# Transposing packed pairs of bf16 as 4-byte elements on TensorE, with the DMA transposes moved back there, in an attention and token-mixing kernel

## The chip, the cores and the metric

The kernel runs on one core of one Trainium2 chip. The metric is the device time of one execution in microseconds (us); several executions are timed and the median of all of them is quoted, slow ones included. Executions are sorted into a fast and a slow state by their length and by TensorE's granted clock (0.968 to 1.00 over the runs of this study); only fast ones are compared, unless it is said otherwise. Each batch of experiments has its own runs of the kernel before, on the same chip; their median is 182.5, 182.8 or 183.6 us.

## The reference

Retention with a decaying state per head (4 batches, 8 heads of 64, 768 steps), then a token-mixing block:

```python
for t in range(S):
    state = gamma * state + outer(k[t], v[t])       # per batch and head
    y[t] = scale * q[t] @ state
x = y with the heads side by side                    # [4, 768, 512]
theta = x @ w_theta
y = w_tok_r @ (x * cos(theta)) + w_tok_i @ (x * sin(theta))
u = x + y
out = u + max(u @ w_ch, 0)                           # float32
```

The kernel cuts time into 24 chunks of 128 rows (6 per batch), works on bf16 copies, and computes retention in blocks. It needs five kinds of transpose: of k and q, of the retention output x, of the token weights w, and of u.

## The kernel before

A transpose on TensorE is one matmul with an identity and a copy out of PSUM. k and q lie side by side in one bf16 tile:

```python
def att_T(n):                                  # k, q of a chunk on TensorE
    kq_ps = psum.tile([P, 2 * NP, P], BF, name="kq_ps", tag="tr", bufs=2)
    for i, src in enumerate((s["kb"], s["qb"])):
        for j in range(NP):                    # NP = 4: eight transposes
            nc.tensor.transpose(kq_ps[:, i * NP + j, :], src[:, j * P:(j + 1) * P], ident)
    kqT = work.tile([P, 2 * NP, P], BF, name="kqT", bufs=4)
    nc.vector.tensor_copy(kqT, kq_ps)

def att_T_dma(n):                              # the same by a DMA
    kqT = work.tile([P, 2 * NP, P], BF, name="kqT", bufs=4)
    nc.sync.dma_start_transpose(out=kqT, in_=s["kqb"].rearrange("p a d -> p (a d)"))
```

Two constants choose where a transpose is done. Chunks from `N_DMA` on transpose k, q and x by DMA, row blocks from `M_DMA` on transpose u by DMA; everything earlier is on TensorE:

```python
N_DMA = (B - 1) * nT + 1      # 19 of 24 chunks: 5 kq and 5 x go by DMA
M_DMA = (B - 2) * nT          # 12 of 24 blocks: u of 12..22 goes by DMA
```

The end is a routine of its own. With u by DMA, the loop runs the product `moe_O` one slot late, so the routine has to add it for blocks 21 and 22:

```python
def moe_last(m):              # m = 23
    ...
    moe_U_dma(m - 1)          # transpose u of block 22
    prods(0)                  # first half of block 23's token mix
    moe_O(m - 2)              # output product of block 21
    prods(1)
    flip(0); moe_O(m - 1); flip(1)
    ...                       # 8 products of 256 columns, two outputs
```

The main loop takes one chunk and one or two half groups of token-mix products (`moe_M`, six 512-column products each) per slot.

Of the kernel before, what the change touches and what calls it, by code (L numbers as in the profile page):

```python
# [32 lines left out]
def kernel(  # L33
# [17 lines left out]
    nc = tc.nc  # L51
# [10 lines left out]
    N_DMA = (B - 1) * nT + 1  # L62
    M_DMA = (B - 2) * nT
# [64 lines left out]
    ident = const.tile([P, P], BF)  # L128
# [13 lines left out]
    wT = [const.tile([P, nT, S], BF, name="wtr"), const.tile([P, nT, S], BF, name="wti")]  # L142
# [4 lines left out]
    def att_prep(n):  # L147
        c = n % nT
        r3 = "p (h d) -> p h d"
        kqb = work.tile([P, 2, dm], BF, name="kqb", bufs=5)  # L150
        kb, qb = kqb[:, 0, :], kqb[:, 1, :]
# [8 lines left out]
    def att_T(n):  # L160
        s = st[n]
        kq_ps = psum.tile([P, 2 * NP, P], BF, name="kq_ps", tag="tr", bufs=2)
        for i, src in enumerate((s["kb"], s["qb"])):
            for j in range(NP):
                nc.tensor.transpose(kq_ps[:, i * NP + j, :],  # L165
                                    src[:, j * P:(j + 1) * P], ident)
        kqT = work.tile([P, 2 * NP, P], BF, name="kqT", bufs=4)
        nc.vector.tensor_copy(kqT, kq_ps)  # L168
        s["kqT"] = kqT

    def att_T_dma(n):
        s = st[n]
        kqT = work.tile([P, 2 * NP, P], BF, name="kqT", bufs=4)
        nc.sync.dma_start_transpose(
            out=kqT, in_=s["kqb"].rearrange("p a d -> p (a d)"))
        s["kqT"] = kqT

    def att_A(n):
        s = st[n]
        kqT = s["kqT"]  # L180
        at_ps = psum.tile([P, 2, NP, P], FT, name="at_ps", tag="at", bufs=1)
        for j in range(NP):
            for par in range(2):
                rows = slice(par * D, (par + 1) * D)
                nc.tensor.matmul(at_ps[:, par, j, :], kqT[rows, j, :],  # L185
                                 kqT[rows, NP + j, :], start=(j == 0),
                                 stop=(j == NP - 1), skip_group_check=True)
# [9 lines left out]
    def att_Yinter(n):  # L197
# [3 lines left out]
        if c > 0:  # L201
            for j in range(NP):
                nc.tensor.matmul(s["yT_ps"][:, j, :], stbd[c % 2][:, j, :],  # L203
                                 s["kqT"][:, NP + j, :], start=(j == 0), stop=False,
                                 skip_group_check=True)

    def att_Y(n):
# [22 lines left out]
        xT = work.tile([P, NP, P], BF, name="xT", bufs=3)  # L230
        nc.scalar.copy(xT, yT_ps)  # L231
# [6 lines left out]
    def att_X_dma(n):  # L238
        b, c = divmod(n, nT)
        nc.sync.dma_start_transpose(  # L240
            out=xs[b][:, c, :].rearrange("p (j e) -> p j e", j=NP),
            in_=st[n]["xT"].rearrange("p j t -> p (j t)"))

    def att_X(n):
        b, c = divmod(n, nT)
        s = st[n]
        if n < N_DMA:
            x_ps = psum.tile([P, NP, P], BF, name="x_ps", tag="tr", bufs=2)
            for j in range(NP):
                nc.tensor.transpose(x_ps[:, j, :], s["xT"][:, j, :], ident)  # L250
        th_ps = psum.tile([P, dm], FT, name="th_ps", tag="acc", bufs=2)
        for j in range(NP):
            nc.tensor.matmul(th_ps, s["xT"][:, j, :], wth[:, j, :], start=(j == 0),  # L253
                             stop=(j == NP - 1))
        if n < N_DMA:
            nc.vector.tensor_copy(xs[b][:, c, :], x_ps.rearrange("p j e -> p (j e)"))
# [14 lines left out]
    def moe_M(m, lo, hi):  # L271
# [8 lines left out]
        for s0 in range(lo, hi):  # L280
            for r in range(2):
                nc.tensor.matmul(y_ps, wT[r][:, s0, t0 * P:(t0 + 1) * P],  # L282
# [7 lines left out]
    def moe_U(m):  # L290
        u_ps = psum.tile([P, nD, P], BF, name="u_ps", tag="tr", bufs=2)
        for j in range(nD):
            nc.tensor.transpose(u_ps[:, j, :], mo[m]["u"][:, j * P:(j + 1) * P], ident)
        uT = work.tile([P, nD, P], BF, name="uT", bufs=3)
        nc.scalar.copy(uT, u_ps)
        mo[m]["uT"] = uT

    def moe_U_dma(m):
        uT = work.tile([P, nD, P], BF, name="uT", bufs=3)
        nc.sync.dma_start_transpose(out=uT, in_=mo[m]["u"])  # L300
        mo[m]["uT"] = uT

    def moe_O(m):
        b, t0 = divmod(m, nT)
        if m >= M_DMA:
# [212 lines left out]
```

## Time and profile before

| | before |
|---|---|
| time, median of 3 runs | 182.69 us (182.03 to 184.78) |
| span of the profiled run | 181.8 us |
| TensorE busy over the span | 157.7 us, 87% |
| transposes on TensorE / by DMA | 352 / 21 |
| stretch to 59 us | loads set the pace, TensorE busy 40.5 us |
| 59 us to some 176 us | TensorE full |

The views that this rests on are in the prediction. Three more lines, of the groups of instructions on the page, are below. Columns: line, engine, operation, out<-in, shape and type, count; then busy us, mean ns of one; then idle time of the engine just before them and what ended most of it.

```profile
L165 PE MATMUL kq_ps<-ident,kqb 128*128 128x128 bf16 x152 | 13.6, 234 | 11.1 <-POOL kqb L153 7.0
L153 POOL CAST kqb<-kf 128x512 bf16<-128x512 f32 x24 | 16.0, 667 | 19.9 <-DMA kf<-in_k_dram 14.1
L231 ACT CAST xT<-yT_ps 128x512 bf16<-128x512 f32 x24 | 14.1, 586 | 19.4 <-PE yT_ps L214 18.1
```

The 234 ns of the first line is the duration of one instruction and not the pace, which the prediction reads from starts.

### The profile page before, as it was taken

To read this page: it belongs to the slowest core of one execution; us is meant where nothing else is said; L and a number is where in the kernel's file an instruction comes from. 1 tells how busy PE (TensorE), PEld (TensorE's weight loads), DVE (VectorE), ACT (ScalarE), POOL (GpSimd) and SP (SyncE) were. 2 spreads that over 40 slices of the span, in tenths; PEclk is the share of its full clock that TensorE was granted. 3 is DMA by queue.
4 is the path that set the end of the run, shared out by engine and by line. 5 is a ranking of instruction groups with operands and counts; after the bars stand their busy time and mean duration, and the time that the engine had idled before them with its cause. 6 is when DMAs were issued, how large, how long until landed. Compare 5 with 4: busy or idle time off the path is not lost.

```text
span 181.8 us, 3528 instructions
## 1 busy us (share of the span) xinstructions
PE 157.7 (87%) x1367; PEld 90.7 (50%) x1392; DVE 104.8 (58%) x146; ACT 74.7 (41%) x140; POOL 79.9 (44%) x104
## 2 busy tenths in 40 slices
PE   0567987897764999999999999999999999999991
PEld 0344655553542655656565565455545544444560
DVE  1264794716822777878676877765645744434442
ACT  4053764821429535647554363356345332200010
POOL 4648677869075768865777847250000000000000
PEclk9999999999999999999999999999999999999997
DMA  6999999999998999999999989984483333334433
GB/s 128 222 316 218 224 276 259 294 288 231 227 259 180 260 243 225 222 272 271 223 228 251 266 208 233 263 151 115 119 112 102 103 97 90 104 93 110 132 105 117
DMA packets 95265, 35.63 MB, mean 196 GB/s; under 512 B 89488, under 2 KB 89744, under 8 KB 95248
## 3 DMA queue, kind: packets, MB, share of 16 engines
q1 hardware_dynamic: 95104, 35.27, 86.4%
q8 instruction: 11, 0.18, 0.5%
q10 hardware_dynamic: 144, 0.13, 0.2%
q14 instruction: 6, 0.05, 0.1%
HBM read 25.69 MB, written 6.29 MB: 176 GB/s over the span
## 4 chain that ended last, share of the span: by engine, by line
PE 62%; SPq 18%; DMA 12%; issue 2%; POOL 2%; DVE 1%; DVEq 0%
PE y_ps L282 27%; SPq L80 15%; PE o_ps L310 11%; PE th_ps L253 8%; DMA kf<-in_k_dram 4%; DMA qf<-in_q_dram 3%; PE yT_ps L214 3%; DMA wtok<-in_moe_w_tok_r_dram 3%; PE at_ps L185 3%; PE kq_ps L165 3%; PE st_ps L222 2%; SPq L94 2%; DMA uT<-u 2%; PE yT_ps L203 2%; PE x_ps L250 1%
## 5 line engine op out<-in xcount | busy, mean ns | idle before, releaser
L282 PE MATMUL y_ps<-z,wti 128*128 128x512 bf16 x137 | 51.9, 379 | 1.6 <-ACT wti L332 0.9
L282 PE MATMUL y_ps<-z,wtr 128*128 128x512 bf16 x125 | 47.4, 379 | 0.7 <-DVE u L287 0.3
L189 DVE TENSOR_TENSOR at<-at_ps,mask 128x1024 bf16<-128x1024 f32 x24 | 29.3, 1220 | 8.9 <-PE at_ps L185 8.8
L258 ACT ACTIVATE cs<-th_ps,halfpi 128x512 bf16<-128x512 f32 x24 | 16.5, 688 | 38.0 <-PE th_ps L253 34.1
L154 POOL TENSOR_TENSOR kqb<-qf,qsc 128x512 bf16<-128x512 f32 x24 | 25.7, 1071 | 11.3 <-DMA qf<-in_q_dram 11.1
L156 POOL TENSOR_TENSOR vb<-vf,vsc 128x512 bf16<-128x512 f32 x24 | 25.9, 1081 | 7.0 <-DMA vf<-in_v_dram 5.8
L264 DVE TENSOR_TENSOR z<-cs,x_sb 128x1024 bf16<-128x1024 bf16 x24 | 19.6, 818 | 14.2 <-ACT cs L259 14.2
L168 DVE COPY kqT<-kq_ps 128x1024 bf16<-128x1024 bf16 x19 | 13.1, 691 | 24.6 <-PE kq_ps L165 24.4
L253 PE MATMUL th_ps<-wth,xT 128*128 128x512 bf16 x89 | 24.4, 387 | 2.4 <-DVE wth L395 1.9
L153 POOL CAST kqb<-kf 128x512 bf16<-128x512 f32 x24 | 16.0, 667 | 19.9 <-DMA kf<-in_k_dram 14.1
L310 PE MATMUL o_ps<-wch,uT 128*128 128x512 bf16 x88 | 23.1, 379 | 0.4 <-DMA uT<-u 0.2
L165 PE MATMUL kq_ps<-ident,kqb 128*128 128x128 bf16 x152 | 13.6, 234 | 11.1 <-POOL kqb L153 7.0
L287 DVE TENSOR_TENSOR u<-y_ps,x_sb 128x512 bf16<-128x512 f32 x23 | 15.8, 690 | 11.9 <-PE y_ps L282 11.9
L313 DVE SCALAR_TENSOR_TENSOR ot<-o_ps,u 128x512 f32<-128x512 f32 x23 | 15.9, 692 | 10.7 <-PE o_ps L310 10.7
L231 ACT CAST xT<-yT_ps 128x512 bf16<-128x512 f32 x24 | 14.1, 586 | 19.4 <-PE yT_ps L214 18.1
L282 PEld LDWEIGHTS <-wti 128*128 128x128 bf16 x138 | 13.5, 98 | 15.4 <-issue 1.9
L282 PEld LDWEIGHTS <-wtr 128*128 128x128 bf16 x138 | 13.5, 98 | 13.5
L165 PEld LDWEIGHTS <-kqb 128*128 128x128 bf16 x152 | 10.6, 104 | 16.5 <-POOL kqb L153 7.9
L259 ACT ACTIVATE cs<-th_ps,zerob 128x512 bf16<-128x512 f32 x24 | 16.3, 681 | 0.0
L236 ACT CAST stbd<-st_ps 64x256 bf16<-64x256 f32 x40 | 14.7, 366 | 0.5
L310 PEld LDWEIGHTS <-uT 128*128 128x128 bf16 x92 | 8.8, 98 | 10.3 <-DMA uT<-u 0.4
L253 PEld LDWEIGHTS <-xT 128*128 128x128 bf16 x96 | 8.8, 100 | 9.2 <-issue 2.6
(51 smaller groups left out, 147.3 us busy)
## 6 DMA issues: line engine op xcount, KB each, us to landing
kf<-in_k_dram SPq DMA_DIRECT2D x24, 256.0 KB, 4.9
qf<-in_q_dram SPq DMA_DIRECT2D x24, 256.0 KB, 5.0
vf<-in_v_dram SPq DMA_DIRECT2D x24, 256.0 KB, 5.3
out_dram<-ot SPq DMA_DIRECT2D x23, 256.0 KB, 2.2
wtok<-in_moe_w_tok_r_dram SPq DMA_DIRECT2D x6, 384.0 KB, 5.3
wtok<-in_moe_w_tok_i_dram SPq DMA_DIRECT2D x6, 384.0 KB, 5.9
w<-in_moe_w_theta_dram SPq DMA_DIRECT2D x1, 1024.0 KB, 6.7
w<-in_moe_w_ch_dram SPq DMA_DIRECT2D x1, 1024.0 KB, 7.8
```

The lines of the kernel that those rows point to most:

```text
L80: nc.sync.dma_start(out=t, in_=src[b, :, c * P:(c + 1) * P, :].rearrange("h s d -> s h d"))
L153: nc.gpsimd.tensor_copy(kb.rearrange(r3, h=H), raw[n, "kf"])
L154: nc.gpsimd.tensor_mul(qb.rearrange(r3, h=H), raw[n, "qf"], _bcast_last(qsc[:, c], D))
L156: nc.gpsimd.tensor_mul(vb.rearrange(r3, h=H), raw[n, "vf"], _bcast_last(vsc[:, c], D))
L165: nc.tensor.transpose(kq_ps[:, i * NP + j, :], src[:, j * P:(j + 1) * P], ident)
L189: nc.vector.tensor_mul(at.rearrange("p a j t -> p (a j) t"), at_ps.rearrange("p a j t -> p (a j) t"), _bcast_mid(mask, H))
L253: nc.tensor.matmul(th_ps, s["xT"][:, j, :], wth[:, j, :], start=(j == 0), stop=(j == NP - 1))
L258: nc.scalar.activation(cs[:, 0, :], th_ps, AF.Sin, bias=halfpi, scale=1.0)
L259: nc.scalar.activation(cs[:, 1, :], th_ps, AF.Sin, bias=zerob, scale=1.0)
L264: nc.vector.tensor_mul(zs[b][:, c], st[n]["cs"], _bcast_mid(xs[b][:, c, :], 2))
L282: nc.tensor.matmul(y_ps, wT[r][:, s0, t0 * P:(t0 + 1) * P], zs[b][:, s0, r, :], start=(s0 == 0 and r == 0), stop=(s0 == nT - 1 and r == 1))
L310: nc.tensor.matmul(o_ps, mo[m]["uT"][:, j, :], wch[:, j, :], start=(j == 0), stop=(j == nD - 1))
```

## The change

Intent: a 4-byte element can carry two bf16 values through a transpose, so half as many transposes do the same work. k and q are interleaved (`[P, dm, 2]`), reinterpreted as float32 and transposed by four instructions instead of eight; x, w and u are packed likewise. Products then read their bf16 operands with a step of two. All 21 DMA transposes return to TensorE.

```diff
-    N_DMA = (B - 1) * nT + 1
-    M_DMA = (B - 2) * nT
...
-    ident = const.tile([P, P], BF)
+    ident = const.tile([P, P], FT)
...
-        kqb = work.tile([P, 2, dm], BF, name="kqb", bufs=5)
-        kb, qb = kqb[:, 0, :], kqb[:, 1, :]
+        kqb = work.tile([P, dm, 2], BF, name="kqb", bufs=5)
+        kb, qb = kqb[:, :, 0], kqb[:, :, 1]
...
     def att_T(n):
-        kq_ps = psum.tile([P, 2 * NP, P], BF, name="kq_ps", tag="tr", bufs=2)
-        for i, src in enumerate((s["kb"], s["qb"])):
-            for j in range(NP):
-                nc.tensor.transpose(kq_ps[:, i * NP + j, :],
-                                    src[:, j * P:(j + 1) * P], ident)
+        kq_ps = psum.tile([P, NP, P], FT, name="kq_ps", tag="tr", bufs=2)
+        for j in range(NP):
+            nc.tensor.transpose(kq_ps[:, j, :],
+                                s["kqb"][:, j * P:(j + 1) * P, :].rearrange(
+                                    "p c i -> p (c i)").bitcast(FT), ident)
+        kqT = work.tile([P, NP, P, 2], BF, name="kqT", bufs=4)
...
+        s["kT"] = [kqT[:, j, :, 0] for j in range(NP)]
+        s["qT"] = [kqT[:, j, :, 1] for j in range(NP)]
-    def att_T_dma(n):
...
-    def att_X_dma(n):
...
-    def moe_U_dma(m):
...
     def moe_last(m):
-        moe_U_dma(m - 1)
+        moe_U(m - 1)
         prods(0)
         moe_O(m - 2)
...
-        if 1 < U_at.get(s_, M_DMA) < M_DMA:
+        if U_at.get(s_, 0) > 1:
             moe_O(U_at[s_])
```

(x, w and u are cut; they follow the same pattern. The cast of w_theta is split between VectorE and ScalarE.) The last two hunks together have a side effect: `moe_O` now runs in the same slot as its transpose, also for block 21, and `moe_last` still runs it a second time.

More of the change, by code (lines that the diff above doesn't have):

```diff
@@ L141 @@
     wch = const.tile([P, nD, dm], BF)
-    wT = [const.tile([P, nT, S], BF, name="wtr"), const.tile([P, nT, S], BF, name="wti")]
+    wT = [const.tile([P, nT, nT // 2, P, 2], BF, name="wtr"),
+          const.tile([P, nT, nT // 2, P, 2], BF, name="wti")]
     st = {}
@@ L161, in att_T @@
         s = st[n]
-        kq_ps = psum.tile([P, 2 * NP, P], BF, name="kq_ps", tag="tr", bufs=2)
-        for i, src in enumerate((s["kb"], s["qb"])):
-            for j in range(NP):
-                nc.tensor.transpose(kq_ps[:, i * NP + j, :],
-                                    src[:, j * P:(j + 1) * P], ident)
-        kqT = work.tile([P, 2 * NP, P], BF, name="kqT", bufs=4)
-        nc.vector.tensor_copy(kqT, kq_ps)
-        s["kqT"] = kqT
-    def att_T_dma(n):
-        s = st[n]
-        kqT = work.tile([P, 2 * NP, P], BF, name="kqT", bufs=4)
-        nc.sync.dma_start_transpose(
-            out=kqT, in_=s["kqb"].rearrange("p a d -> p (a d)"))
-        s["kqT"] = kqT
+        kq_ps = psum.tile([P, NP, P], FT, name="kq_ps", tag="tr", bufs=2)
[4 more added lines that the diff above has]
+        kqT = work.tile([P, NP, P, 2], BF, name="kqT", bufs=4)
+        nc.vector.tensor_copy(kqT.rearrange("p j t i -> p (j t i)"),
+                              kq_ps.rearrange("p j t -> p (j t)").bitcast(BF))
+        s["kT"] = [kqT[:, j, :, 0] for j in range(NP)]
+        s["qT"] = [kqT[:, j, :, 1] for j in range(NP)]
     def att_A(n):
         s = st[n]
-        kqT = s["kqT"]
         at_ps = psum.tile([P, 2, NP, P], FT, name="at_ps", tag="at", bufs=1)
@@ L184, in att_A @@
                 rows = slice(par * D, (par + 1) * D)
-                nc.tensor.matmul(at_ps[:, par, j, :], kqT[rows, j, :],
-                                 kqT[rows, NP + j, :], start=(j == 0),
+                nc.tensor.matmul(at_ps[:, par, j, :], s["kT"][j][rows],
+                                 s["qT"][j][rows], start=(j == 0),
                                  stop=(j == NP - 1), skip_group_check=True)
@@ L203, in att_Yinter @@
                 nc.tensor.matmul(s["yT_ps"][:, j, :], stbd[c % 2][:, j, :],
-                                 s["kqT"][:, NP + j, :], start=(j == 0), stop=False,
+                                 s["qT"][j], start=(j == 0), stop=False,
                                  skip_group_check=True)
@@ L229, in att_Y @@
             zs[b] = big.tile([P, nT, 2, dm], BF, name="z")
-        xT = work.tile([P, NP, P], BF, name="xT", bufs=3)
-        nc.scalar.copy(xT, yT_ps)
+        xT = work.tile([P, NP // 2, P, 2], BF, name="xT", bufs=3)
+        nc.scalar.copy(xT.rearrange("p a t b -> p a b t"),
+                       yT_ps.rearrange("p (b a) t -> p a b t", b=2))
         s["xT"] = xT
@@ L236, in att_Y @@
                 nc.scalar.copy(stbd[(c + 1) % 2][sl, :, sl], st_ps[b][sl, :, sl])
-    def att_X_dma(n):
-        b, c = divmod(n, nT)
-        nc.sync.dma_start_transpose(
-            out=xs[b][:, c, :].rearrange("p (j e) -> p j e", j=NP),
-            in_=st[n]["xT"].rearrange("p j t -> p (j t)"))
     def att_X(n):
@@ L246, in att_X @@
         s = st[n]
-        if n < N_DMA:
-            x_ps = psum.tile([P, NP, P], BF, name="x_ps", tag="tr", bufs=2)
-            for j in range(NP):
-                nc.tensor.transpose(x_ps[:, j, :], s["xT"][:, j, :], ident)
+        x_ps = psum.tile([P, NP // 2, P], FT, name="x_ps", tag="tr", bufs=2)
+        for a in range(NP // 2):
+            nc.tensor.transpose(x_ps[:, a, :],
+                                s["xT"][:, a].rearrange(
+                                    "p t i -> p (t i)").bitcast(FT), ident)
         th_ps = psum.tile([P, dm], FT, name="th_ps", tag="acc", bufs=2)
         for j in range(NP):
-            nc.tensor.matmul(th_ps, s["xT"][:, j, :], wth[:, j, :], start=(j == 0),
-                             stop=(j == NP - 1))
-        if n < N_DMA:
-            nc.vector.tensor_copy(xs[b][:, c, :], x_ps.rearrange("p j e -> p (j e)"))
+            nc.tensor.matmul(th_ps, s["xT"][:, j % 2, :, j // 2], wth[:, j, :],
+                             start=(j == 0), stop=(j == NP - 1))
+        nc.vector.tensor_copy(xs[b][:, c, :],
+                              x_ps.rearrange("p a e -> p (a e)").bitcast(BF))
         cs = work.tile([P, 2, dm], BF, name="cs", bufs=2)
@@ L281, in moe_M @@
             for r in range(2):
-                nc.tensor.matmul(y_ps, wT[r][:, s0, t0 * P:(t0 + 1) * P],
+                nc.tensor.matmul(y_ps, wT[r][:, t0, s0 % (nT // 2), :, s0 // (nT // 2)],
                                  zs[b][:, s0, r, :], start=(s0 == 0 and r == 0),
@@ L290, in moe_U @@
     def moe_U(m):
-        u_ps = psum.tile([P, nD, P], BF, name="u_ps", tag="tr", bufs=2)
-        for j in range(nD):
-            nc.tensor.transpose(u_ps[:, j, :], mo[m]["u"][:, j * P:(j + 1) * P], ident)
-        uT = work.tile([P, nD, P], BF, name="uT", bufs=3)
-        nc.scalar.copy(uT, u_ps)
-        mo[m]["uT"] = uT
-    def moe_U_dma(m):
-        uT = work.tile([P, nD, P], BF, name="uT", bufs=3)
-        nc.sync.dma_start_transpose(out=uT, in_=mo[m]["u"])
-        mo[m]["uT"] = uT
+        u_ps = psum.tile([P, nD // 2, P], FT, name="u_ps", tag="tr", bufs=2)
+        for a in range(nD // 2):
+            nc.tensor.transpose(u_ps[:, a, :],
+                                mo[m]["u"][:, 2 * a * P:2 * (a + 1) * P].bitcast(FT),
+                                ident)
+        uT = work.tile([P, nD // 2, P, 2], BF, name="uT", bufs=3)
+        nc.scalar.copy(uT.rearrange("p a t i -> p (a t i)"),
+                       u_ps.rearrange("p a t -> p (a t)").bitcast(BF))
+        mo[m]["uT"] = [uT[:, j % 2, :, j // 2] for j in range(nD)]
     def moe_O(m):
         b, t0 = divmod(m, nT)
-        if m >= M_DMA:
-            o_ps = psum.tile([P, dm], FT, name="o_ps", tag="tr", bufs=2)
-        else:
-            o_ps = psum.tile([P, dm], FT, name="o_ps", tag="acc", bufs=2)
+        o_ps = psum.tile([P, dm], FT, name="o_ps", tag="acc", bufs=2)
         for j in range(nD):
-            nc.tensor.matmul(o_ps, mo[m]["uT"][:, j, :], wch[:, j, :], start=(j == 0),
+            nc.tensor.matmul(o_ps, mo[m]["uT"][j], wch[:, j, :], start=(j == 0),
                              stop=(j == nD - 1))
         ot = work.tile([P, dm], FT, name="ot", bufs=4)
-        nc.vector.scalar_tensor_tensor(ot, o_ps, 0.0, mo[m]["u"], ALU.max, ALU.add)
+        nc.vector.scalar_tensor_tensor(
+            ot.rearrange("p (b r) -> p b r", b=2),
+            o_ps.rearrange("p (b r) -> p b r", b=2), 0.0,
+            mo[m]["u"].rearrange("p (r b) -> p b r", b=2),
+            ALU.max, ALU.add)
         nc.sync.dma_start(out=out[b, t0 * P:(t0 + 1) * P, :], in_=ot)
@@ L320, in w_cast @@
             row = work.tile([P, S], BF, name="wrow", bufs=3)
-            nc.gpsimd.tensor_copy(row, wdma[r, t0])
+            nc.gpsimd.tensor_copy(
+                row.rearrange("p (i b) -> p b i", b=2),
+                wdma[r, t0].rearrange("p (b i) -> p b i", b=2))
             wrow[r, t0] = row
@@ L325, in w_tok @@
         for r in range(2):
-            w_ps = psum.tile([P, nT, P], BF, name="w_ps", tag="tr", bufs=2)
-            for s0 in range(nT):
-                nc.tensor.transpose(w_ps[:, s0, :],
-                                    wrow[r, t0][:, s0 * P:(s0 + 1) * P], ident)
-            dst = wT[r][:, :, t0 * P:(t0 + 1) * P]
+            w_ps = psum.tile([P, nT // 2, P], FT, name="w_ps", tag="tr", bufs=2)
+            for a in range(nT // 2):
+                nc.tensor.transpose(
+                    w_ps[:, a, :],
+                    wrow[r, t0][:, 2 * a * P:2 * (a + 1) * P].bitcast(FT), ident)
+            dst = wT[r][:, t0].rearrange("p a t b -> p (a t b)")
+            src = w_ps.rearrange("p a t -> p (a t)").bitcast(BF)
             if r:
-                nc.scalar.copy(dst, w_ps)
+                nc.scalar.copy(dst, src)
             else:
-                nc.vector.tensor_copy(dst, w_ps)
+                nc.vector.tensor_copy(dst, src)
     def moe_last(m):
@@ L342, in moe_last @@
         u = work.tile([P, dm], BF, name="u", bufs=4)
-        uT = work.tile([P, nD, P], BF, name="uT", bufs=3)
+        uT = work.tile([P, nD // 2, P, 2], BF, name="uT", bufs=3)
         def prods(e):
@@ L347, in prods @@
                 for r in range(2):
-                    nc.tensor.matmul(y_ps[e], wT[r][:, s0, t0 * P:(t0 + 1) * P],
+                    nc.tensor.matmul(y_ps[e], wT[r][:, t0, s0 % (nT // 2), :, s0 // (nT // 2)],
                                      zs[b][:, s0, r, e * hw:(e + 1) * hw],
@@ L355, in flip @@
         def flip(e):
-            u_ps = psum.tile([P, 2, P], BF, name="u_ps", tag="tr", bufs=2)
-            for j in range(2):
-                jj = 2 * e + j
-                nc.tensor.transpose(u_ps[:, j, :], u[:, jj * P:(jj + 1) * P], ident)
-            nc.scalar.copy(uT[:, 2 * e:2 * e + 2, :], u_ps)
-        moe_U_dma(m - 1)
+            u_ps = psum.tile([P, P], FT, name="u_ps", tag="tr", bufs=2)
+            nc.tensor.transpose(u_ps, u[:, e * hw:(e + 1) * hw].bitcast(FT), ident)
+            nc.scalar.copy(uT[:, e].rearrange("p t i -> p (t i)"), u_ps.bitcast(BF))
+        moe_U(m - 1)
         prods(0)
@@ L370, in moe_last @@
                 psum.tile([P, hw], FT, name="o_ps", tag="acc", bufs=2)]
-        for js in ((0, 1), (2, 3)):
+        for js in ((0, 2), (1, 3)):
             for e in range(2):
                 for j in js:
-                    nc.tensor.matmul(o_ps[e], uT[:, j, :],
+                    nc.tensor.matmul(o_ps[e], uT[:, j % 2, :, j // 2],
                                      wch[:, j, e * hw:(e + 1) * hw], start=(j == 0),
@@ L378, in moe_last @@
             ot = work.tile([P, hw], FT, name="oh", bufs=2)
-            nc.vector.scalar_tensor_tensor(ot, o_ps[e], 0.0, u[:, e * hw:(e + 1) * hw],
-                                           ALU.max, ALU.add)
+            nc.vector.scalar_tensor_tensor(
+                ot, o_ps[e], 0.0, u.rearrange("p (r b) -> p b r", b=2)[:, e],
+                ALU.max, ALU.add)
             (nc.sync, nc.scalar)[e].dma_start(
@@ L394 @@
         if n == 1:
-            nc.vector.tensor_copy(wth, wdma["th"])
+            nc.vector.tensor_copy(
+                wth[:, :nD // 2].rearrange("p d (r b) -> p d b r", b=2),
+                wdma["th"][:, :nD // 2].rearrange("p d (b r) -> p d b r", b=2))
+            nc.scalar.copy(
+                wth[:, nD // 2:].rearrange("p d (r b) -> p d b r", b=2),
+                wdma["th"][:, nD // 2:].rearrange("p d (b r) -> p d b r", b=2))
         if n > 0:
@@ L445 @@
             load_chunk(n + 5)
-        if U_at.get(s_, 0) >= M_DMA:
-            moe_U_dma(U_at[s_])
-        if n is not None and nT < n < N_DMA:
+        if n is not None and n > nT:
             att_T(n)
@@ L458 @@
             w_cast(3 + s_ // 2)
-        if s_ + 1 in n_of and n_of[s_ + 1] < N_DMA:
+        if s_ + 1 in n_of:
             att_prep(n_of[s_ + 1])
-        if s_ + 2 in n_of and n_of[s_ + 2] >= N_DMA:
-            att_prep(n_of[s_ + 2])
-            att_T_dma(n_of[s_ + 2])
         if s_ in (1, 3, 5):
             w_tok(3 + s_ // 2)
-        if U_at.get(s_ - 1, 0) >= M_DMA:
-            moe_O(U_at[s_ - 1])
         if s_ - 1 in n_of:
             att_Yinter(n_of[s_ - 1])
-        if U_at.get(s_, M_DMA) < M_DMA:
+        if s_ in U_at:
             moe_U(U_at[s_])
@@ L475 @@
             att_Y(n_of[s_ - 1])
-            if n_of[s_ - 1] >= N_DMA:
-                att_X_dma(n_of[s_ - 1])
         if s_ == 2:
```

## The prediction

> **What bounds the kernel now.** I read the page first (the tenths by slice, then the chain that ended last), then the busy time by stretches, then TensorE's instructions in order of time around 100 us, then the last ten microseconds. The slices:
>
> ```profile
> PE   0567987897764999999999999999999999999991
> DMA  6999999999998999999999989984483333334433
> ```
>
> A slice is 4.5 us. Until slice 13, some 59 us, TensorE (PE) has holes and the DMA engines are full; from then on TensorE is full to the end. The stretches say it in numbers (stretch, length, busy PE, PEld, DVE, ACT, POOL, granted clock, DMA share, GB/s):
>
> ```profile
> 0.00:59.00 59.00, 40.50 (x415) 25.16 (x422) 29.79 (x42) 27.02 (x50) 37.66 (x60) 1.00 1.06 240
> 59.00:80.00 21.00, 20.43 (x218) 12.91 (x221) 15.72 (x23) 11.52 (x22) 15.90 (x17) 1.00 1.12 243
> 100.00:120.00 20.00, 19.74 (x191) 11.68 (x193) 15.02 (x19) 9.42 (x18) 10.10 (x11) 1.00 1.15 230
> 140.00:160.00 20.00, 19.90 (x119) 9.52 (x120) 9.43 (x13) 6.47 (x12) 0.00 (x0) 1.00 0.34 93
> ```
>
> TensorE is busy 40.5 of the first 59 us and over 97% after; no other engine passes 75% there. The chain in order of time agrees: up to 58.9 us it is loads and their issue, with GpSimd's casts between, and afterwards nearly only products:
>
> ```profile
> 51.51 6.18 DMA qf<-in_q_dram
> 57.76 1.05 POOL kqb L154
> 58.86 0.41 PE kq_ps L165 x4
> ```
>
> So the time is about 59 us of loading, which TensorE's savings can't shorten, then about 118 us in which each TensorE nanosecond counts, then about 4 us for the last output. Loads stay ahead in the second part: the query cast started at 95.71 us on GpSimd is first transposed near 111 us.
>
> What a transpose costs is read from starts, not from the durations in the groups, since those include a pipeline that the next instruction overlaps. TensorE in order of time:
>
> ```profile
> 97.17 0.39 PE L250 MATMUL x_ps<-ident,xT 128*128 128x128 bf16 x4
> 97.39 1.03 PE L253 MATMUL th_ps<-wth,xT 128*128 128x512 bf16 x4
> 98.26 0.61 PE L165 MATMUL kq_ps<-ident,kqb 128*128 128x128 bf16 x8
> 98.70 0.38 PE L282 MATMUL y_ps<-z,wtr 128*128 128x512 bf16 x1
> 98.92 0.38 PE L282 MATMUL y_ps<-z,wti 128*128 128x512 bf16 x1
> ```
>
> Eight transposes take 98.70 - 98.26 = 0.44 us, four take 0.22 us: 55 to 56 ns each. A 512-column product takes 98.92 - 98.70 = 0.22 us (0.216 over six of them).
>
> [...]
> 1. [...] each 4-byte transpose became one weight load and one matmul.
> 2. [...] The trace shows the size: 98 ns for a 128-column bf16 load and 109 ns for a 64-column one (line 214, 100 to 135 us). [...]
> 3. [...] the 56 ns pace is what the path pays.
> 4. [...] No line of this trace shows a stepped operand on TensorE.
>
> **The change part by part.** The built programs' instruction lists give the counts.
>
> *Transposes on TensorE.* Before: 152 kq + 76 x + 72 w + 52 u = 352, plus 21 DMA transposes (5 kq, 5 x, 11 u). After: 96 + 48 + 36 + 48 = 228. Only those after 59 us count. Before, by the time order: 9 chunks x 8 kq (72), 12 x 4 x (48), 24 w, 10 x 4 u (40), 4 at the end: 188, x 56 ns = 10.5 us. After: 14 x 4 kq (56), 17 x 2 x (34), 12 w, 21 x 2 u (42), 2 at the end: 146. If c is the cost of one 4-byte transpose, the difference is 146c - 10.5 us:
> - c = 58 ns, my choice [...]: 8.5, saving 2.0 us.
> - c = 110 ns (load and matmul one after the other): 16.1, costing 5.6 us.
> - [...]
>
> Halving the count on the chunks that were on TensorE is therefore mostly eaten by the chunks that come back from the DMA.
>
> *The DMA transposes.* All are issued from 110 us on, when the last loads go out and the DMA share falls from 1.15 to 0.34. The DMA had room and TensorE hid them, so removing them gives nearly nothing except at one place, the end:
>
> ```profile
> 171.92 0.76 PE y_ps L348 x7
> 172.67 3.02 DMA uT<-u
> 175.69 0.04 issue
> 175.73 0.39 PE o_ps L310
> ```
>
> The chain passes through that 3.02 us, but TensorE worked beside most of it; its list of instructions shows 0.22 us idle before the product at 175.73 (0.39 us for the weight load).
>
> *The end, rebuilt.* Reading the new order I found three things. (a) The output product of row block 21 is run twice: once in the last slot of the loop, once in the last-block routine. The list has 96 of these products against 92: 4 x 0.216 = +0.86 us of TensorE. (b) The transpose of block 22 now stands in front of the last block's products and needs u, ready near 172.65, while TensorE gets there near 172.6: +0.1 to +0.2 with its two transposes. (c) The product of block 22 now takes an accumulator of the pool that holds the last block's second half, so it waits for VectorE's add: in the kernel before that add ended 0.73 us after the last such product started. TensorE would arrive after 0.17: a wait of about 0.6 in place of about 0.4. Sum: about +1.2 us.
>
> *Stepped operands.* In y, th and o the stepped operand is the stationary one, hidden behind 0.216 us. Only the attention products stream a stepped operand (8 of at and 4 of yT per chunk), and I take them as free. The stepped writes on GpSimd and ScalarE I take at the old durations (0.61 and 1.04 us; 0.59 us). VectorE and ScalarE gain 5 kq copies of 0.69, 5 x copies of 0.41 and 11 u copies of 0.59 us after 110 us, where they are under 60% busy: beside other work.
>
> *Sum.* 182.7 - 2.0 + 1.2 = 181.9; I add 0.7 for transposes that show their weight load at the head of a group (some 60 groups after 59 us, an estimate of 12 ns each). **Predicted: 182.6 us.**
>
> **The rivals.**
> 1. *The 4-byte transpose is slow.* For it: [...] no trace here. Against: one instruction pair in the built program[...]. 110 ns makes 189.5 us[...]. The largest doubt.
> 2. *The stepped stream halves TensorE's rate on N=128 products.* The yT group with kqT would go from 0.22 to 0.44 us, and at by some 0.1: +0.3 us on 15 chunks, +5 us, 187 us. For: twice the bytes are spanned. [...]
> 3. *GpSimd becomes the bound through 2-byte writes at a step of four bytes.* It is 76% busy from 59 to 80 us. Casts 50% longer would add 0.8 us per chunk, and 0.8 us to the last wait for a load at 59 us: 183 to 186 us. Nothing in the profile speaks for it.
> 4. *The DMA was the hidden bound and its relief shows.* The chain's DMA share of 12% speaks for it at first sight; but that is loads before 59 us, which the change leaves alone, and one piece at the end. At most -0.5 us.
>
> **Range and chances.** Within 2% is 179.0 to 186.3 us. With the other terms as above, 186.3 needs c of about 80 to 85 ns. I give c below that two chances in three; the stepped operands and GpSimd take a little from it. Being under 179.0 would need 3.7 us, more than all that the faster transposes can give while (a) stands. So faster 0.06, same 0.62, slower 0.32; range 180.0 to 193.0, long above because rival 1 has a tail there.
>
> **What would show it.** In the changed profile: starts of x_ps transposes about 58 ns apart (two in 0.12, four kq in 0.23 us); attention groups still 0.33 us for eight and 0.22 for four; GpSimd casts still 0.61 and 1.04 us; TensorE full from 59 us; 96 products of 512 columns into o_ps; a wait on VectorE before the product of block 22. I am wrong if four kq transposes take over 0.4 us, if at or yT groups lengthen, if a stretch after 59 us has TensorE under 95% with GpSimd or ScalarE as releaser, or if the loading stretch ends clearly before or after 59 us.

## The result, and the profile after

All ratios here are the mean time of one kernel's fast runs over the mean of the other's fast runs of the same rounds, so they are not quite the ratio of the quoted medians.

| | before | after |
|---|---|---|
| time, median | 182.74 us (182.03 to 184.78, 4 runs) | 188.3 us (187.44 to 190.12, 4 runs) |
| ratio, 95% interval | | 1.031 (1.022 to 1.041): slower |
| span of the profiled run | 181.8 us | 186.1 us |
| TensorE busy | 157.7 us | 164.9 us |
| GpSimd busy | 79.9 us | 85.3 us |
| ScalarE busy | 74.7 us | 84.9 us |
| DMA packets | 95,265 | 81,424 |

The slices of the changed kernel:

```profile
PE   0378898796886999999999999999999999999993
DMA  6999999999999999999999988111011011113114
```

TensorE fills up at about the same slice as before, and stays full. The DMA engines now stand almost idle in the last 40% of the run, and the time is longer. Its stretches:

```profile
0.00:59.00 59.00, 43.08 (x347) 26.59 (x353) 30.56 (x44) 29.34 (x51) 42.42 (x61) 1.00 1.14 250
59.00:80.00 21.00, 19.65 (x176) 12.28 (x178) 15.81 (x23) 11.90 (x21) 16.62 (x17) 1.00 1.14 245
140.00:160.00 20.00, 19.89 (x129) 10.95 (x130) 10.94 (x18) 8.79 (x15) 0.00 (x0) 1.00 0.14 53
```

From 59 us no engine but TensorE passes 80% of a stretch, as before. One hole of TensorE is larger than before: in the stretch from 59 to 80 us it is 93.6% busy, where it was 97.3%. Its transposes of u at 60.66 us had waited 1.19 us for VectorE's copy of a token weight; before, that wait was 0.35 us. No loss shows at the end of this stretch: in profiles with the full clock there, chunk 12 starts at 77.5 to 78.1 us with the packed layout (after, e1, e2, e4) and at 77.0 to 78.9 us with the plain one (before, e6, e7). So the question is what TensorE does with the time. Its instructions in order of time, in the same phase of a slot as the lines quoted before:

```profile
97.17 0.60 PE L163 MATMUL kq_ps<-ident,kqb 128*128 128x128 f32 x4
97.61 0.38 PE L271 MATMUL y_ps<-z,wtr 128*128 128x512 bf16 x1
...
98.91 0.39 PE L196 MATMUL yT_ps<-kqT,stbd 128*128 128x128 bf16 x4
99.14 0.39 PE L282 MATMUL u_ps<-ident,u 128*128 128x128 f32 x2
99.45 0.40 PE L178 MATMUL at_ps<-kqT 64*128 64x128 bf16 x8
99.79 0.41 PE L207 MATMUL yT_ps<-at,vb 128*64 128x128 bf16 x8
```

Four 4-byte transposes take 97.61 - 97.17 = 0.44 us: 110 ns each, and exactly the time of the eight 2-byte ones before. The attention products with their stepped operands have kept their time: 99.14 - 98.91 = 0.23 us for four of yT, 99.79 - 99.45 = 0.34 us for eight of at. A whole slot at this place is unchanged too: kq transposes start at 97.17 and 103.61 us, 6.44 us apart; before at 98.26 and 104.69, 6.43 us.

The groups that answer to those shown of before:

```profile
L163 PE MATMUL kq_ps<-ident,kqb 128*128 128x128 f32 x96 | 16.0, 293 | 8.8 <-POOL kqb L153 8.8
L152 POOL CAST kqb<-kf 128x512 bf16<-128x512 f32 x24 | 19.6, 815 | 19.4 <-DMA kf<-in_k_dram 12.1
L224 ACT CAST xT<-yT_ps 128x512 bf16<-128x512 f32 x24 | 17.8, 741 | 14.1 <-PE yT_ps L207 12.5
```

Writing bf16 with a step of two made GpSimd's cast of k longer by 148 ns and ScalarE's copy of x by 155 ns, each 24 times. That is real work, but it lies beside TensorE's.

The last ten microseconds of the changed kernel (TensorE, its weight loads and VectorE):

```profile
176.85 0.20 PEld L282 LDWEIGHTS u_ps<-ident,u 128*128 128x128 f32 x2 [0.41 <-DVE u L276]
...
178.43 1.03 PE L294 MATMUL o_ps<-wch,uT 128*128 128x512 bf16 x4
...
180.72 1.03 PE L294 MATMUL o_ps<-wch,uT 128*128 128x512 bf16 x4
180.81 0.42 DVE L344 TENSOR_TENSOR u<-y_ps,x_sb 128x256 bf16<-128x256 f32 x1 [0.62 <-PE y_ps L340]
...
181.69 1.24 PE L364 MATMUL o_ps<-wch,uT 128*128 128x256 bf16 x8
```

The products at 178.43 us are block 21's second time. The transpose of block 22 waited for u, as foreseen. The products of block 22 at 180.72 us started before VectorE's add at 180.81, so they did not wait for it, which the prediction had expected.

**A ruler inside the trace.** Run times mix the loading stretch, which differs from profile to profile (chunk 12's attention products start anywhere from 77.0 to 80.3 us in the profiles), with the part that the change acts on. So I also measure, in each profile, from the start of chunk 12's attention products to the start of the last block's eight 256-column products:

| profile | chunk 12 | last products | distance | against before |
|---|---|---|---|---|
| before | 78.85 | 176.72 | 97.87 | |
| after | 77.76 | 181.69 | 103.93 | +6.06 |
| after, run again | 77.51 | 181.44 | 103.93 | +6.06 |

The span grew by 4.3 us only, as the profiled run came out of loading 1.1 us earlier (78.85 to 77.76) and its tail after these products is 0.7 us shorter (5.1 to 4.4); the distance is what the change did to the full part of TensorE. It can be taken apart: 5 kq, 5 x and 11 u that were DMA transposes are now 20 + 10 + 22 = 52 transposes of 110 ns, +5.72; the second product of block 21, four times 0.216, +0.86; a DMA wait of 0.39 us at the end gone, a wait of 0.08 us for u added. The sum is +6.27, against 6.06 measured. Four further waits of some 0.08 us in the kernel before, described with e7, are gone as well; with them the sum is +5.94. Either way the sum is within 0.2 us of the measurement, and nothing is left over for a gain from packing.

### The profile page after: what moved, and what is told of

Same layout as the page of the kernel before. It is cut to its first block, busy times and chain, and to the rows that moved or that the text cites.

```text
span 186.1 us, 3289 instructions
## 1 busy us (share of the span) xinstructions
PE 164.9 (89%) x1250; PEld 97.3 (52%) x1272; DVE 110.1 (59%) x157; ACT 84.9 (46%) x152; POOL 85.3 (46%) x104
## 2 busy tenths in 40 slices
DMA packets 81424, 32.46 MB, mean 174 GB/s; under 512 B 75520, under 2 KB 75776, under 8 KB 81408
## 4 chain that ended last, share of the span: by engine, by line
PE 80%; ACT 6%; DVE 6%; DMA 3%; issue 2%; SPq 1%; POOL 1%; DVEq 0%
PE y_ps L271 31%; PE o_ps L294 11%; PE th_ps L242 11%; PE kq_ps L163 5%; PE yT_ps L207 4%; PE at_ps L178 4%; PE st_ps L215 3%; PE u_ps L282 3%; PE x_ps L237 3%; DMA qf<-in_q_dram 3%; PE yT_ps L196 2%; DVE z L253 2%; SPq L78 1%; ACT cs L247 1%; PE y_ps L340 1%
## 5 line engine op out<-in xcount | busy, mean ns | idle before, releaser
L167 DVE COPY kqT<-kq_ps 128x1024 bf16<-128x1024 bf16 x24 | 16.6, 690 | 24.8 <-PE kq_ps L163 24.8
L153 POOL TENSOR_TENSOR kqb<-qf,qsc 128x512 bf16<-128x512 f32 x24 | 25.9, 1081 | 7.1 <-DMA qf<-in_q_dram 6.8
L152 POOL CAST kqb<-kf 128x512 bf16<-128x512 f32 x24 | 19.6, 815 | 19.4 <-DMA kf<-in_k_dram 12.1
L242 PE MATMUL th_ps<-wth,xT 128*128 128x512 bf16 x92 | 25.1, 391 | 1.7 <-DVE wth L386 1.3
L286 ACT COPY uT<-u_ps 128x512 bf16<-128x512 bf16 x23 | 13.5, 586 | 28.5 <-PE u_ps L282 28.5
L294 PE MATMUL o_ps<-wch,uT 128*128 128x512 bf16 x94 | 24.2, 379 | 0.1
L224 ACT CAST xT<-yT_ps 128x512 bf16<-128x512 f32 x24 | 17.8, 741 | 14.1 <-PE yT_ps L207 12.5
L163 PE MATMUL kq_ps<-ident,kqb 128*128 128x128 f32 x96 | 16.0, 293 | 8.8 <-POOL kqb L153 8.8
L163 PEld LDWEIGHTS kq_ps<-ident,kqb 128*128 128x128 f32 x96 | 12.4, 150 | 13.8 <-POOL kqb L153 10.2
L297 DVE SCALAR_TENSOR_TENSOR ot<-o_ps,u 128x512 f32<-128x512 f32 x24 | 16.6, 692 | 5.0 <-PE o_ps L294 4.9
L309 POOL CAST wrow<-wtok 128x768 bf16<-128x768 f32 x12 | 13.1, 1100 | 5.0 <-PE w_ps L318 1.9
```

The lines of the kernel that those rows point to most:

```text
L152: nc.gpsimd.tensor_copy(kb.rearrange(r3, h=H), raw[n, "kf"])
L153: nc.gpsimd.tensor_mul(qb.rearrange(r3, h=H), raw[n, "qf"], _bcast_last(qsc[:, c], D))
L163: nc.tensor.transpose(kq_ps[:, j, :], s["kqb"][:, j * P:(j + 1) * P, :].rearrange("p c i -> p (c i)").bitcast(FT), ident)
L167: nc.vector.tensor_copy(kqT.rearrange("p j t i -> p (j t i)"), kq_ps.rearrange("p j t -> p (j t)").bitcast(BF))
L224: nc.scalar.copy(xT.rearrange("p a t b -> p a b t"), yT_ps.rearrange("p (b a) t -> p a b t", b=2))
L242: nc.tensor.matmul(th_ps, s["xT"][:, j % 2, :, j // 2], wth[:, j, :], start=(j == 0), stop=(j == NP - 1))
```

## The experiments

**e1: the changed kernel again**, unchanged, five rounds.

> The changed kernel again, as the yardstick of this chip: 1.025 to 1.035 times the kernel before (187 to 189 us). It is the run that the next two are compared with.

Measured: 189.07 us, two of six runs slow; ratio 1.033 (1.026 to 1.040). The result stands.

**e2: the second product taken out.**

```diff
         prods(0)
-        moe_O(m - 2)
         prods(1)
```

> The changed kernel without the second run of block 21's output product. If the four products of 0.216 us are on the path, as the list of TensorE's instructions says: 0.86 us less than the changed kernel (187.4 us against 188.3). If they lie in a wait that would be there anyway (TensorE waits at the end for VectorE's add): less than 0.3 us less.

Measured: 187.47 us, two of six runs slow; ratio 1.026 (1.022 to 1.030). The distance in the trace is 78.01 to 181.07 = 103.06 us: 0.87 us shorter than after, for four products of 0.216 us = 0.86. By the clock alone, the two intervals overlap; the trace settles the size.

**e3: the kernel before, with every transpose on TensorE as 2-byte elements.** This is the change without packing and without stepped operands.

```diff
-    N_DMA = (B - 1) * nT + 1
-    M_DMA = (B - 2) * nT
+    N_DMA = B * nT
+    M_DMA = B * nT
...
-        moe_U_dma(m - 1)
+        moe_U(m - 1)
         prods(0)
-        moe_O(m - 2)
```

> The kernel before with no DMA transposes: 2-byte transposes on TensorE everywhere, plain layouts, the block order of the changed kernel, no second product. Theory 'packing gains nothing, since one 4-byte transpose takes as long as two 2-byte ones; the loss is the 21 transposes that come back from the DMA': equal to the run without the second product within 0.8 us (about 187.4 us). Rival 'the interleaved layout costs': the stepped writes on GpSimd (815 against 667 ns) and ScalarE (741 against 586 ns) hold the path, so this run is at least 2 us faster than the one without the second product (185.4 or less). Rival 'packing does help somewhere, before 59 us for instance': this run is at least 1.5 us slower than it.

Measured: 187.38 us, ratio 1.028 (1.023 to 1.032), against e2's 187.47 us and 1.026 on the same chip. The ends of the ruler, e2's two lines first, then e3's:

```profile
78.01 0.40 PE L178 MATMUL at_ps<-kqT 64*128 64x128 bf16 x8
181.07 1.24 PE L363 MATMUL o_ps<-wch,uT 128*128 128x256 bf16 x8
79.76 0.40 PE L185 MATMUL at_ps<-kqT 64*128 64x128 bf16 x8
182.83 1.24 PE L373 MATMUL o_ps<-wch,uT 128*128 128x256 bf16 x8
```

The distance is 182.83 - 79.76 = 103.07 us, and e2's is 103.06. (In the profile of e3 the clock was lower before chunk 12: 0.95 from 55 to 60 us and 0.71 from 60 to 65 us.) The two kernels differ in every transpose, in the layout of k, q, x, w and u, and in GpSimd's and ScalarE's writes, and their TensorE timelines have the same length. So packing gains nothing, the new layout costs nothing on the path, and the whole loss beside the second product comes from taking the transposes back from the DMA: 40 + 20 + 44 = 104 two-byte transposes of 55 ns are 5.72 us, less the 0.39 us of DMA wait 5.33; measured 5.20 (with the smaller waits described with e7, the sum is 5.1).

**e4: the disputed cost by itself.** Into e2's kernel, at slot 12, I put rows of like instructions on data that lie ready: 12 transposes of each kind, and 8 products.

```diff
+        f4 = wth[:, 0, :2 * P].bitcast(FT)
+        b2 = wth[:, 1, :P]
+        step = wth[:, 2, :2 * P] as bf16 with a step of two; wide = 512 columns likewise
+        A: transpose(p1[:, k % 4, :], f4, ident)                    # float32, 128x128
+        B: transpose(p2[:64, k % 4, :], f4[:, :64], ident)          # 64 columns of data
+        G: transpose(p7[:, k % 4, :64], f4[:64], ident[:64, :64])   # 64 rows of data
+        C: transpose(p3[:, k % 4, :], b2, identb)                   # bf16
+        D: transpose(p4[:, k % 4, :], b2, identw[:, :, 0])          # identity with a step of two
+        E: transpose(p5[:, k % 4, :], step, identb)                 # data with a step of two
+        F: matmul(p6, b2, wide)                                     # moving operand with a step
```

(Condensed: the letters stand for loops, and the making of the tiles and of the bf16 identities is cut.) The data are the stationary operand and the identity is the moving one, so B halves the weight load and leaves the moving columns at 128, and G halves the moving columns and leaves a weight load of 128 columns.

> Blocks of twelve equal transposes put into the kernel of the second run, after the slot that is at about 120 us, to read their pace; the time itself does not matter (some 7 us more). 4-byte 128x128: 110 ns each, as in the changed kernel. What the 110 ns are: H1, the 4-byte identity streams at half rate: with 64 data columns (weight load half as long, stream as long) 107 to 110 ns, with 64 data rows (stream half as long) 55 ns. H2, the weight load is not hidden and adds to a stream of 56 ns: 80 ns in both. H3, the weight load alone takes 107 ns and bounds: 55 ns with 64 columns, 110 ns with 64 rows. 2-byte, plain: 56 ns; with a stepped identity (moving operand at a step of two): 56 ns if a stepped stream is free, 107 if it halves the rate; with stepped data as weights: 56 ns [...]. 512-column product with a stepped moving operand: 216 ns if free, about 430 if not.

Measured (one run, of unknown state, granted clock 1.00), TensorE in order of time:

```profile
116.64 1.47 PE L432 MATMUL pA_f<-ident,wth 128*128 128x128 f32 x12
117.95 1.47 PE L435 MATMUL pB_f_64cols<-ident,wth 128*64 128x128 f32 x12
119.36 0.97 PE L438 MATMUL pG_f_64rows<-ident,wth 64*128 64x64 f32 x12
120.25 0.84 PE L441 MATMUL pC_bf<-identb,wth 128*128 128x128 bf16 x12
120.94 0.86 PE L444 MATMUL pD_bf_stepmoving<-identw,wth 128*128 128x128 bf16 x12
121.63 0.83 PE L447 MATMUL pE_bf_stepweights<-identb,wth 128*128 128x128 bf16 x12
122.30 1.97 PE L450 MATMUL pF_bf_prod_step<-wth 128*128 128x512 bf16 x8
```

The single starts inside each row, from the trace, lie apart by: A 109 ns, B 109, G 63, C 56, D 58, E 56, F 226. Halving the weight load (B) brings nothing; halving the moving columns (G) brings the time to 63 ns. The weight loads themselves confirm that B did halve something:

```profile
L432 PEld LDWEIGHTS pA_f<-ident,wth 128*128 128x128 f32 x12 | 1.4, 140 | 0.2
L435 PEld LDWEIGHTS pB_f_64cols<-ident,wth 128*64 128x64 f32 x12 | 1.3, 111 | 0.0
L438 PEld LDWEIGHTS pG_f_64rows<-ident,wth 64*128 64x128 f32 x12 | 0.8, 140 | 0.2 <-issue 0.2
```

140 ns became 111 ns in B, and the pace stayed. In G the load kept its 140 ns, and yet a transpose started every 63 ns. So the time of a 4-byte transpose follows the columns that stream: 109 ns over 128 columns is 0.85 ns a column, against 0.42 ns for bf16 (216 ns over 512 in this kernel), a factor of two. The weight load does not set it. A step of two costs bf16 nothing on the stationary side (E 56 for C's 56) and next to nothing on the moving one: 58 ns for 56, and 226 for 216 over 512 columns, under 5%. Whether the factor comes from the 4-byte moving operand or from the 4-byte output, this run doesn't separate, since a transpose changes both together. G also halves the rows together with the moving columns, and its 63 ns are 8 above half of 109; 64 moving columns with all 128 rows were not tried.

**e5: the changed kernel with k and q of the last five chunks unpacked and by DMA again.**

```diff
+        if n >= N_DMA:
+            flat = kqb.rearrange("p c i -> p (c i)")
+            kb, qb = flat[:, :dm], flat[:, dm:]
...
+    def att_T_dma(n):
+        nc.sync.dma_start_transpose(out=flat, in_=s["kqb"].rearrange("p c i -> p (c i)"))
```

(Shortened: the second `flat` is a plain view of the tile kqT. As in the kernel before, these chunks are prepared two slots ahead.)

> The changed kernel with one kind of DMA transpose given back: k and q of chunks 19 to 23 are kept unpacked and transposed by the DMA, as before the change; everything else as changed. Theory 'what came back from the DMA is the loss': 5 chunks x 4 x 0.11 us = 2.2 us less than the changed kernel (186.1 us). Rival 'the DMA transposes were no gain, the layout is the loss': under 0.5 us less.

Measured: median 187.6 us over six runs, of which three were slow; the three fast ones took 185.6, 185.9 and 186.6 us, ratio 1.019 (1.014 to 1.024), which leaves open on which side of 2% it lies. The profiled run was slow, but its lower clock lies before chunk 12 (0.71 from 60 to 65 us, 0.95 from 65 to 70 us); its distance is 101.67 us, 2.26 less than after. Twenty transposes of 110 ns are 2.20 us. The DMA does hide them.

**e6 and e7: the two parts of the return, one at a time, in the kernel before.** e6 takes only u back to TensorE, e7 only k, q and x, both as 2-byte elements.

```diff
# e6: M_DMA = B * nT, moe_U(m - 1) in place of moe_U_dma(m - 1), no moe_O(m - 2)
# e7: N_DMA = B * nT
```

(The edits in short, not the diff itself.)

> The kernel before with the u transposes of blocks 12 to 22 on TensorE (2-byte), k, q and x still by DMA. Theory: 11 x 4 x 0.056 = 2.4 us more, less the wait of up to 0.4 us for the last DMA transpose that goes: about +2.1 us, 184.8 us. If the end's wait was worth more than the 0.4 us that TensorE stood idle: under +1 us.

> The kernel before with k, q and x of chunks 19 to 23 on TensorE (2-byte), u still by DMA. Theory: 5 x 8 x 0.056 + 5 x 4 x 0.056 = 3.4 us more, about 186.1 us. Together with the run for u it should add up to the run with all on TensorE. Rival 'those DMA transposes cost waits of their own in the middle': under +2 us.

Measured: e6 183.21 us, ratio 1.005 (1.001 to 1.010), distance 99.79 us, +1.92; e7 184.53 us, ratio 1.011 (1.006 to 1.016), distance 100.52 us, +2.65. Worked out from the pace of 55 ns: e6 44 x 55 ns = 2.42, less 0.39 of DMA wait, 2.03; e7 60 x 55 ns = 3.30. e6 is 0.11 us below its sum. e7 is 0.65 us short of it, and the two parts add to 4.57 us where e3 shows 5.20 us.

The traces show where e7 found 0.65 us: in two kinds of wait that the kernel before has and e7 has not. First, the DMA wait of 0.39 us at the end is gone: in e7 the product of block 22 starts at 177.80 us, 0.11 us after the two transposes at 177.69. Second, the kernel before loses some 0.08 us in each of four slots after 130 us: TensorE has only four products of th to do before the next block's first product, which needs the accumulator y_ps, and VectorE's add is still reading that. One of the four: the add runs from 138.74 to 139.43 us, the last th product starts at 139.19, and the next y_ps product starts at 139.48, 0.30 us later where the pace is 0.22. In e7 the transposes of k and q stand in between. The two kinds make 0.39 + 0.33 = 0.72 us. e6 and e7 each lose the end wait, and e6 loses three of the four small waits too, so adding the two counts some 0.6 us twice.

The wait at the end also differs between profiles of an unchanged end: 0.39 us in the kernel before, 0.30 in e9, 0.80 in e10. The ruler carries this difference.

**e8: more by DMA instead of less.** If each transpose on TensorE costs its 55 ns, moving more of them to the DMA should gain.

```diff
-    N_DMA = (B - 1) * nT + 1
-    M_DMA = (B - 2) * nT
+    N_DMA = 17
+    M_DMA = 9
```

> The other direction: the kernel before with more transposes by DMA, from chunk 17 instead of 19 for k, q and x, and from block 9 instead of 12 for u. If a transpose is worth its time on TensorE wherever TensorE is full: 2 x 12 x 0.056 + 3 x 4 x 0.056 = 2.0 us less than the kernel before (180.7 us). Rival 'while the loads still fill the DMA engines (share 1.15 until about 114 us), a DMA transpose comes late and TensorE waits for it': no gain, or a loss.

Measured: 186.92 us, ratio 1.021 (1.016 to 1.026): no gain but a loss, of which the interval leaves open whether it passes 2%. Two of six runs, and the profiled one, are slow, so the profile is read for a cause only and not compared in length. It shows TensorE first, the queue of the issuing engine after it:

```profile
122.06 1.89 PE L310 MATMUL o_ps<-wch,uT 128*128 128x512 bf16 x4 [4.45 <-DMA uT<-u]
123.88 0.61 PE L185 MATMUL at_ps<-kqT 64*128 64x128 bf16 x8
```

```profile
116.63 1.03 SPq L80 DMA_DIRECT2D vf<-in_v_dram  x1
117.76 2.13 SPq L300 DMA_TRANSPOSE uT<-u  x1
```

The product of a row block waited 4.45 us for a DMA transpose that was issued only after a chunk's loads had been issued on the same queue, and then took 4.25 us to land while loads filled the DMA engines (share 1.22 from 100 to 120 us). Afterwards TensorE ran slower: eight attention products from 123.88 to 124.42 us are 0.54 us, where they take 0.33 us, and the granted clock was 0.56 between 120 and 125 us and 0.75 between 125 and 130. Here one gap of 4.45 us was followed by some 5 us at the low clock; whether the gap lowered the clock, this one profile doesn't show. So the boundary in the kernel before, the first DMA transposes at the time when the last loads go out, looks well placed; the DMA share falls only from then on (1.27 from 110 to 120 us, 0.43 from 120 us to the end). I tried one setting beyond it, so this doesn't show that 19 and 12 are the best ones.

**e9 and e10: TensorE's work moved into the loading stretch.** If TensorE's own work after 59 us sets the time, work moved in front of it must come off the end. In e9 one half group (1.29 us) goes from behind the wait for chunk 9 to in front of it; in e10 both halves of that block go one place earlier.

```diff
 # e9
+    halves[2], halves[3] = [(3, 0, nT // 2), (3, nT // 2, nT)], []
 # e10
+    halves[1].append((3, 0, nT // 2))
+    halves[2], halves[3] = [None, (3, nT // 2, nT)], []
 # both
-        if hs:
+        if hs and hs[0]:
             moe_M(*hs[0])
```

> The kernel before, with one half of a token-mix product group (six 512-column products, 1.29 us of TensorE) moved from behind the wait for chunk 9 to in front of it, where the trace of the kernel before shows TensorE idle for 1.49 and 0.97 us. Nothing is added or removed. If TensorE's own work after 59 us sets the time (my theory, which also makes the 4-byte transposes cost what they stream), 1.29 us less of it there ends the program 1.2 to 1.3 us earlier: about 181.4 us, ratio 0.993, and the distance from the attention products of chunk 12 to the last block shrinks little or by that amount, depending on where the loading stretch ends. If a transfer or GpSimd paced the chunks after 59 us as well (the rival), nothing is gained: 182.7 us.

> The same with both halves of that block moved one place earlier, so that a half group also stands in front of the wait for chunk 8 (idle 0.71 and 1.01 us in the kernel before). By my theory the second move gains nothing on top if chunk 9's arrival ends the stretch in any case (the work that was between the two waits is only moved forward within the loading stretch), so again about 181.4 us; it would show more only if the work before chunk 9 was late for its load.

Measured: e9 182.19 us, ratio 0.995 (0.987 to 1.002); e10 181.84 us, ratio 0.994 (0.987 to 1.000); the kernel before took 183.63 us in these rounds, with a wide spread (182.56 to 187.0). The trace of e9 shows the hole getting smaller:

```profile
56.32 0.39 PE L165 MATMUL kq_ps<-ident,kqb 128*128 128x128 bf16 x4
57.30 0.40 PE L165 MATMUL kq_ps<-ident,kqb 128*128 128x128 bf16 x4 [0.60 <-POOL kqb L154]
```

0.60 us idle before chunk 9, where it was 1.49 and 0.97. The distances are 97.78 and 98.28 us, where before's is 97.87; less the wait for the last DMA transpose (0.30, 0.80 and 0.39 us) all three are 97.5 us, so the move left the stretch after chunk 12 as it was. Chunk 12 starts at 76.98 and 77.09 us, earlier than before's 78.85, but other kernels with an unchanged loading stretch also show 77.0 (e6). So the times (medians 1.4 and 1.8 us lower, means of the fast runs 1.0 and 1.2) point as the theory says, but the intervals reach 1: a gain of the expected size is likely and not shown. These are the only versions with a median below that of the kernel before.

One more idea wasn't run, transposes of the type float32r.

## Why the prediction was right or wrong

The measured time, 188.3 us, lies inside the range of 180 to 193 us, in its upper half: the point was 182.6 us, 5.7 us too low, and "within 2%", which I had given 0.62, did not come; "slower" had 0.32. That the range holds the result is owed to the tail kept for the first rival; the main reading failed. Point by point:

1. **What bounds the kernel: right in the main.** TensorE is full after 59 us in the kernel before; other engines reach 75.7% there (the prediction said that none passes 75%). In the changed kernel the first stretch is at 93.6%, below the 95% that the prediction had set as a sign of being wrong, but VectorE is the releaser. e2, e3, e5 and e6 each change TensorE's work after 59 us, and the distance follows within 0.15 us; so does e7 once the waits that it removes are counted. e9 and e10, which only move work, point the same way without deciding.
2. **The cost of one 4-byte transpose: wrong, and this is the step that failed.** The prediction chose "c = 58 ns, my choice". It is 109 to 110 ns, and the sign that the prediction had set, four kq transposes over 0.4 us, came with 0.44. For the count of 146 against 188 transposes after 59 us that turns a saving of 2.0 us into a cost of 5.6 us: 7.6 us, more than the whole error. Points 5 (c) and 8, costs that did not come, took some 1.3 us back. The first rival named 110 ns, and that is what came, with 189.5 us for the whole, 1.2 us too high; but the reason that the prediction gave for 110 ns, "load and matmul one after the other", is wrong as well. e4 shows that halving the weight load changes nothing (109 ns) and halving the moving columns does (63 ns): the 4-byte stream runs at half rate (0.85 ns a column against 0.42). The 58 ns was my estimate and no trace showed it. I could have seen that the number I needed stood in none, and weighed it evenly: with half rate and full rate at like odds the point would have been near 186 us.
3. **"Halving the count on the chunks that were on TensorE is therefore mostly eaten": too kind.** At twice the time for half the count, packing is exactly neutral (e2 against e3: 103.06 and 103.07 us), and the transposes that come back from the DMA are a pure loss of about 5.2 us.
4. **The DMA transposes hidden, except one place at the end: right in the main.** e3, e5 and e6 confirm it within 0.15 us; e7 fell 0.65 us short of its sum and so pointed to four small waits in the kernel before, 0.33 us together, that the prediction had not seen.
5. **The end.** (a) The second product of block 21: right, 0.87 us for 0.86. (b) The wait for u came, with 0.08 us of TensorE. The prediction's 0.1 to 0.2 took in the block's two transposes, which its count of 146 already had; wait and transposes together took 0.35 us. (c) A wait of 0.6 us on VectorE before the product of block 22: wrong. It started at 180.72 us, 0.51 us before the add that was to release its accumulator ended (180.81 + 0.42 = 181.23), so it had another buffer. I had inferred the buffer from the pool's order; why it got another one, no run shows. The old DMA wait went without a successor.
6. **Stepped operands free on TensorE: right, nearly.** at and yT keep their times (0.34 and 0.23 us); e4 finds 2 ns on a stepped stream of 128 columns and 10 ns on one of 512, a form that this kernel doesn't have. The second rival, half rate, falls.
7. **Stepped writes at the old durations: wrong in size, without effect.** GpSimd's cast of k took 815 ns for 667, its cast of w 1100 for 960, ScalarE's copy of x 741 for 586. The third rival was right that they cost something and wrong about the path: GpSimd is busy 16.62 us of the 21 after 59 us, and e2 with these writes ends its distance with e3 without them.
8. **The 0.7 us for heads of groups: not seen.** The 12 ns a group was an estimate for which the prediction named no measured number. The sum in the ruler's section closes within 0.2 us without it.

## What to carry to other kernels

When a change trades the count of instructions for their size, the pace of the larger one decides everything: read it from starts in a trace, and where no trace has it, give half rate and full rate like odds instead of choosing. Before taking work off the DMA because "the chain passes through it", ask whether the bounding engine waited: here 21 DMA transposes came with one wait of 0.39 us and four of 0.08 us of TensorE, and their return cost over 5 us. And separate the two things that a change does by building the one without the other: the unpacked kernel without DMA transposes showed in one run that packing had done nothing at all.

## Paces and durations measured

- A 128x128 transpose starts every 109 ns as float32 and every 56 ns as bf16, in the same run (e4, A and C). A 4-byte transpose streams at half the bf16 rate, so packing two bf16 into it gains nothing (e2 and e3: 103.06 and 103.07 us).
- One bf16 transpose lasts 219 to 220 ns (e4, C to E), and in a row they start 56 to 58 ns apart. For planning, the second number is needed.
- A bf16 weight load of 128 columns took 98 ns with a step of two (E) and without (C); a 4-byte one took 140 ns for 128 columns and 111 ns for 64 (A and B). A moving operand with a step of two: 58 ns for 56 without (D and C), and 226 for 216 with 512 columns (F, and this kernel's products).
- GpSimd's writes of bf16 with a step of 4 bytes, after for before: 815 ns for 667 (cast, 128x512), 1100 ns for 960 (cast, 128x768); a tensor multiply of 128x512 with the same output and step only 1081 ns for 1071.
- One DMA transpose took 1.2 to 3.7 us on the queue of the issuing engine in the kernel before, where plain loads on it took 0.4 to 2.3 us between 100 and 115 us; a transpose issued among loads landed after 4.25 us (e8).
